# Where the second FFN's first weight operand lives, when its last three are fetched, and what is loaded ahead of its second product

## The chip, the cores and the metric

The kernel runs on one core of a Trainium2 chip. The metric is device time in microseconds (us) of one execution, from a set of timed runs; a profiled execution gives the trace. Engines: TensorE (PE, with its weight loads PEld), VectorE (DVE), ScalarE (ACT), GpSimd (POOL) and SyncE (SP). SP and POOL issue the DMAs here, each on a queue of its own.

## The reference, cut to what matters

```python
x = attention(q, k, v)              # linear attention with decay, 4 x 8 heads, 768 tokens, 64 wide
a = x @ w1; b = x @ w2              # first FFN: 3072 tokens, 512 -> 1024
x = ((a * b) @ w3) @ w_out          # 1024 -> 1024 -> 512
h = x @ w_in                        # second FFN: 512 -> 2048
g = h * (1 / (1 + exp(-1.702 * h)))
out = g @ w_out2                    # 2048 -> 512
```

The change touches the second FFN alone: `x @ w_in` with its gate, and `g @ w_out2`.

## The kernel before, in words

Every product is made of three matmuls (`mm3`), of a high and a low part of each operand. Both products of the second FFN are Strassen-like: seven block products P1 to P7 stand for the eight of a 2 x 2 block matrix.

**The block loop ahead of it.** The first FFN runs over six blocks of 512 tokens. In the last block each step f makes the products `gate(f)` (tile psm) and `mixed(f - 1)` (tile acc); `mixed(7)` is the last work. Its four results go through ACT or DVE into tiles st and by SP into DRAM (yd). During that block `operands(0, py)` cuts slice 0 of the tokens into the right operands yh, yl.

**Expand** (`x @ w_in`). Four slices s of 2 x 384 tokens, eight quads j each. Quad j of slice s needs the left operand `left[j]` (all seven weight combinations, 1792 KB, DRAM tensor sp) and makes P1, P5, then P4 of the quad before (`fourth`), then P6, P2, P3, P7: 7 x 6 matmuls. P1, P6, P7 and P4 go one after the other into the same PSUM bank a, and ACT copies the bank out after each (s1, u2, u3; after P4 the gate reads it), so that PE may go on in that bank only after the copy. The gates write the tile g (two buffers); DVE adds three more rows to it, and SP stores the whole of it to DRAM (gd, 1344 KB) in `fourth`. ACT does its work in program order: in a quad s1 copy, late gate g2 of the quad before, s5 copy, gate g1 of the quad before, u2 copy, gate g0, u3 copy, gate b12.

**Contract** (`g @ w_out2`). 21 turns (P1, P2, P6, P5, P3, P7, P4, three token ranges i of 512 each), 48 matmuls a turn. A turn reads its operand from gd in two halves of four k (low), ACT copies the high part of a half (h), DVE subtracts it from the low part. Turns n + 2 are loaded at turn n, the split of turn n + 1 stands behind the matmuls of turn n. Turn 0 (gd of slices 0 and 1) is loaded and split during slice 3 of Expand (`OPENING`), and the first half of turn 1 (slices 1 and 2) is loaded in its last quad. The other half of turn 1 is the first line of `contract`. Turn 2 needs all of gd of slice 3.

**Memory**, in bytes of a partition as the program before is laid out: a pool lays its tags one after another in the order of their first tile, and a tile waits for the tiles that lay there earlier, one by one. wmix of the first FFN 41,088 to 73,856 (read up to `mixed(7)` in every slot from 36,992 to 80,000), weights of `gate(4..7)` 73,856 to 106,624, hh and hl 106,624 to 114,816, tmp and st 114,816 to 123,008 (the last four results lie there until their stores have read them), xh and xl 123,008 to 139,392. The pool f then has eight slots of 14,336 from 8,320: slot 0 and 1 are free early, slots 2, 3 and 4 after `mixed(7)`, 5 and 6 a little ahead of it, slot 7 (108,672 to 123,008) after the stores of st. Left operand n goes to slot `SLOT[n]`, all eight asked for on POOL's queue at the start of Expand. Behind them in f1 lie g (123,008 and 133,760), b12, and the tiles s. In contract the pool f2 takes the place of f1 and of y: its first l1 tile (138,880 to 147,072), for the second half of turn 1, lies on the second g buffer, which the store of the last quad reads.

Of the kernel before, what the change touches and what calls it, by code (L numbers as in the profile page):

```python
# [16 lines left out]
P = 128  # L17
# [4 lines left out]
TB = 512  # L22
# [6 lines left out]
TS = 384  # L29
NS = NT // (2 * TS)  # L30
TU = 256
NQ = DG // (2 * P)
# [9 lines left out]
def tile_kernel(  # L42
# [14 lines left out]
    nc = tc.nc  # L57
# [339 lines left out]
    right = {}  # L397
# [66 lines left out]
    def left_parts(n, name, k):  # L464
        return [left[n][:, w, PART[name], k * P : (k + 1) * P] for w in range(2)]

    class Expand:

        def __init__(self, p, pf, py, ps):
            self.p, self.pf, self.py, self.ps = p, pf, py, ps  # L470
# [28 lines left out]
        def quad(self, s, j, step):  # L499
            a, e, c = (self.bank(x) for x in "aec")  # L500
            g = self.p.tile([P, 7, TS], F32, tag="g", bufs=2, name="g")
            b12 = self.p.tile([P, TS], F32, tag="b", bufs=2, name="b12")
            self.product(a, "P1", s, j, True)
            s1 = self.copy(a, "s1")
            if self.late:
                self.gated(*self.late.pop())
            self.product(e, "P5", s, j, True)
            s5 = self.copy(e, "s5")
            if self.open:
                self.fourth()  # L510
# [12 lines left out]
            self.gated(b12, u2)  # L523
            nc.vector.tensor_tensor(u3, u3, s5, ALU.add)
            self.late.append((g[:, 2], u3))
            nc.vector.tensor_tensor(g[:, 3], b12, g[:, 0], ALU.subtract)
            step(3)
            self.open = a, s, j, g, b12

        def run(self):  # L530
            self.late, self.open = [], None
# [3 lines left out]
            nxt = None  # L535
            for s in range(NS):

                for j in range(NQ):

                    def step(at):  # L540
                        nonlocal nxt
                        more = s + 1 < NS
                        if more and (j, at) == (2, 3):
                            nxt = operands(s + 1, self.py)
                            next(nxt)
                        elif more and (j, at) in NEXT:
                            next(nxt)
                        elif s and (j, at) == (0, 0):
                            next(nxt)
                        if not more and (j, at) in OPENING:  # L550
                            OPENING[j, at](self.pf)

                    self.quad(s, j, step)
            self.gated(*self.late.pop())
            self.fourth()

    NEXT = (4, 3), (5, 1), (5, 3), (6, 3), (7, 0), (7, 1), (7, 2), (7, 3)
# [2 lines left out]
    KH = NQ // 2  # L560
    low, high, ws = {}, {}, {}

    def slot(pf, n, shape, dtype=F32R):
        return pf.tile(shape, dtype, tag=f"op{SLOT[n]}", name=f"o{n}")

    def half_tile(p, kind, h, bufs):
        return p.tile([P, KH, TB], F32R, tag=f"{kind}{h}", bufs=bufs, name=f"{kind}{h}")

    def load_half(n, h, t):
        name, i = turns[n]  # L570
        low[n, h] = t
        at = 0
        while at < TB:
            s, t0 = divmod(i * TB + at, TS)
            m = min(TB - at, TS - t0)
            nc.sync.dma_start(
                t[:, :, at : at + m].bitcast(F32),
                gd[s][:, RIGHT[name], h * KH : (h + 1) * KH, t0 : t0 + m],
            )
            at += m  # L580

    def load_turn(n, p):
        if n < len(turns):
            for h in range(2):
                load_half(n, h, half_tile(p, "l", h, 3))

    def split_half(n, h, t, a=0, b=KH, copy=nc.scalar.copy):
        high[n, h] = t
        x = low[n, h][:, a:b]
        copy(t[:, a:b], x.bitcast(F32))  # L590
        nc.vector.tensor_tensor(x, x.bitcast(F32), t[:, a:b].bitcast(F32), ALU.subtract)  # L591

    def split_turn(n, p):
        if n < len(turns):
            for h in range(2):
                split_half(n, h, half_tile(p, "h", h, 2))

    def load_w(name, w, pf, at):
        t = slot(pf, at, [P, NQ, 256])
        ws.setdefault(name, []).append(t)  # L600
        nc.gpsimd.dma_start(t.bitcast(F32), sw[PART[name], :, w])

    def opening_split(h, a):
        def run(pf):
            if a == 0:
                high[0, h] = slot(pf, 2 + h, [P, KH, TB])
            split_half(0, h, high[0, h], a, a + 1)
        return run

    OPENING = {  # L610
        (1, 3): lambda pf: load_half(0, 0, slot(pf, 0, [P, KH, TB])),
        (2, 3): lambda pf: load_half(0, 1, slot(pf, 1, [P, KH, TB])),
        (5, 1): lambda pf: load_w("P1", 0, pf, 4),
        (6, 1): lambda pf: load_w("P1", 1, pf, 5),
        (7, 1): lambda pf: load_half(1, 0, slot(pf, 6, [P, KH, TB])),
    }
    OPENING |= {
        at: opening_split(n // KH, n % KH)
        for n, at in enumerate(
            ((3, 1), (3, 3), (4, 0), (4, 1), (4, 3), (5, 0), (5, 3), (6, 0))  # L620
        )
    }

    def contract(p, pf, ps):
        load_half(1, 1, half_tile(p, "l", 1, 3))
        w_at = (4, 5), (0, 1)
        u = [slot(pf, 7, [P, 3, 2, TB], F32)]

        def add(out, x, y):
            nc.vector.tensor_tensor(out, x, y, ALU.add)  # L630

        def store(x, h, i, q, value):
# [3 lines left out]
            while at < TB:  # L636
# [4 lines left out]
                nc.sync.dma_start(out[rows, to : to + m], t[:, at : at + m])  # L641
                at += m

        for n, (name, i) in enumerate(turns):
            r = n // 3
            load_turn(n + 2, p)
            if i == 0 and n and r + 1 < 7 or n == 1:
                nxt = turns[n + 3 - i][0]
                for w in range(2):
                    load_w(nxt, w, pf, w_at[(r + 1) % 2][w])  # L650
            if name == "P5" and i == 0:
                u += [slot(pf, x, [P, 3, 2, TB], F32) for x in (2, 3)]
            pq = [ps.tile([P, TB], F32, tag="m", bufs=6, name="m") for _ in range(2)]
            for q in range(2):
                for k in range(NQ):
                    mm3(
                        pq[q],
                        *(t[:, k, q * P : (q + 1) * P] for t in ws[name]),
                        high[n, k // KH][:, k % KH],
                        low[n, k // KH][:, k % KH],  # L660
                        k == 0,
                        k == NQ - 1,
                    )
# [20 lines left out]
    with tc.manual_schedule():  # L684
# [70 lines left out]
        with (  # L755
# [108 lines left out]
            late(*args)  # L864
        first.close()

        with tc.tile_pool(name="f", bufs=1, reuse_waits="tile") as pf:
            with (
                tc.tile_pool(name="f1", bufs=1, reuse_waits="tile") as p1,
                tc.tile_pool(name="psf1", bufs=1, space=PSUM, reuse_waits="tile") as ps1,  # L870
            ):
                Expand(p1, pf, py, ps1).run()
            third.close()
            with (
                tc.tile_pool(name="f2", bufs=1, side="right", reuse_waits="tile") as p2,
                tc.tile_pool(name="psf2", bufs=1, space=PSUM, reuse_waits="tile") as ps2,
            ):
                contract(p2, pf, ps2)


_OUTS = [((DM, NT), "float32")]
# [89 lines left out]
```

## Time and profile before

| what | us |
|---|---|
| median of 3 timed runs (1033.01 to 1040.57) | 1037.22 |
| profiled execution, device time | 1040.05 |
| its span in the trace | 1038.3 |
| PE busy in it | 987.5 |
| block loop's last matmul, start of Expand | 547.65 |
| last matmul of Expand, start of contract | 793.74 |

The device time is 1.75 us more than the span. Times in the rows count from the span's start. The mean granted TensorE clock is 0.988 of full speed (2.4 GHz).

### The profile page before, as it was taken

To read this page: it belongs to the slowest core of one execution; us is meant where nothing else is said; L and a number is where in the kernel's file an instruction comes from. 1 tells how busy PE (TensorE), PEld (TensorE's weight loads), DVE (VectorE), ACT (ScalarE), POOL (GpSimd) and SP (SyncE) were. 2 spreads that over 40 slices of the span, in tenths; PEclk is the share of its full clock that TensorE was granted. 3 is DMA by queue.
4 is the path that set the end of the run, shared out by engine and by line. 5 is a ranking of instruction groups with operands and counts; after the bars stand their busy time and mean duration, and the time that the engine had idled before them with its cause. 6 is when DMAs were issued, how large, how long until landed. Compare 5 with 4: busy or idle time off the path is not lost.

```text
span 1038.3 us, 14825 instructions
## 1 busy us (share of the span) xinstructions
PE 987.5 (95%) x5680; PEld 854.2 (82%) x5680; DVE 649.4 (63%) x1038; ACT 436.9 (42%) x831; POOL 32.1 (3%) x57
## 2 busy tenths in 40 slices
PE   4789999999999999999999899999999699999998
PEld 4568777888888888888889899999998488888886
DVE  4977888856777767733343485866764254645563
ACT  4766554434434343322113445445463332434230
POOL 3110000000000000000000000000000000000000
PEclk9999999999999999999999899999999899999999
DMA  8999654546766767641319847556578978868971
GB/s 323 340 405 351 213 182 151 164 154 205 241 222 232 244 214 224 199 152 41 124 31 407 321 178 256 213 202 230 196 257 293 336 255 279 285 234 281 316 257 58
DMA packets 138806, 240.40 MB, mean 232 GB/s; under 512 B 7024, under 2 KB 111600, under 8 KB 132976
## 3 DMA queue, kind: packets, MB, share of 16 engines
q1 hardware_dynamic: 131968, 184.94, 52.6%
q0 software_dynamic: 6768, 54.53, 13.7%
q8 instruction: 44, 0.72, 0.3%
q14 instruction: 26, 0.21, 0.1%
HBM read 148.21 MB, written 91.23 MB: 231 GB/s over the span
## 4 chain that ended last, share of the span: by engine, by line
PE 80%; DMA 8%; DVE 7%; issue 2%; ACT 2%; POOL 0%; SPq 0%; DVEq 0%; ACTq 0%; POOLq 0%
PE psm L231 8%; PE psm L230 8%; PE psm L229 8%; PE m L230 7%; PE m L231 7%; PE m L229 7%; PE acc L230 4%; PE acc L229 4%; PE acc L231 4%; DMA gd<-g 3%; DMA qkv<-in_qkv_dram 3%; PE a L229 3%; PE a L231 3%; PE a L230 3%; PE e L229 2%
## 5 line engine op out<-in xcount | busy, mean ns | idle before, releaser
L231 PE MATMUL psm<-xh,wl 128*128 128x512 f32 x384 | 149.6, 390 | 1.2 <-DVE wl L119 1.2
L230 PE MATMUL psm<-xl,wh 128*128 128x512 f32 x384 | 149.5, 389 | 0.0
L229 PE MATMUL psm<-xh,wh 128*128 128x512 f32 x384 | 149.5, 389 | 0.0
L229 PE MATMUL m<-h,o 128*128 128x512 f32 x320 | 125.5, 392 | 8.1 <-ACT h L590 8.1
L231 PE MATMUL m<-h,o 128*128 128x512 f32 x320 | 125.0, 391 | 0.0
L230 PE MATMUL m<-l,o 128*128 128x512 f32 x312 | 122.2, 392 | 1.5 <-DVE l L591 1.5
L590 ACT CAST h<-l 128x2048 fp32r<-128x2048 f32 x39 | 74.1, 1912 | 102.0 <-DMA l<-gd 58.4
L591 DVE TENSOR_TENSOR l<-l,h 128x2048 fp32r<-128x2048 f32 x39 | 88.0, 2286 | 35.6 <-ACT h L590 35.5
L801 DVE TENSOR_TENSOR tmp<-tmp,psm 128x512 f32<-128x512 f32 x48 | 32.9, 686 | 103.9 <-PE psm L231 92.9
L229 PE MATMUL a<-yh,op 128*128 128x384 f32 x256 | 87.0, 340 | 8.9 <-ACT u L478 8.9
L230 PE MATMUL a<-yl,op 128*128 128x384 f32 x256 | 86.4, 337 | 0.0
L231 PE MATMUL a<-yh,op 128*128 128x384 f32 x256 | 86.4, 337 | 0.0
L231 PEld LDWEIGHTS psm<-xh,wl 128*128 128x128 f32 x384 | 72.1, 188 | 16.5 <-DVE wl L119 1.6
L229 PEld LDWEIGHTS psm<-xh,wh 128*128 128x128 f32 x384 | 72.1, 188 | 15.0
L230 PEld LDWEIGHTS psm<-xl,wh 128*128 128x128 f32 x384 | 72.1, 188 | 14.9
L782 ACT CAST hh<-tmp 128x512 fp32r<-128x512 f32 x48 | 29.8, 620 | 124.1 <-DVE tmp L801 124.1
L229 PEld LDWEIGHTS m<-h,o 128*128 128x128 f32 x320 | 60.5, 189 | 21.2 <-ACT h L590 8.5
L229 PE MATMUL acc<-hh,wh 128*128 128x512 f32 x192 | 74.7, 389 | 0.0
L230 PE MATMUL acc<-hl,wh 128*128 128x512 f32 x192 | 74.7, 389 | 0.0
L231 PE MATMUL acc<-hh,wl 128*128 128x512 f32 x192 | 74.7, 389 | 0.0
L231 PEld LDWEIGHTS m<-h,o 128*128 128x128 f32 x320 | 60.5, 189 | 12.4
L230 PEld LDWEIGHTS m<-l,o 128*128 128x128 f32 x312 | 59.0, 189 | 14.3 <-DVE l L591 2.0
(109 smaller groups left out, 1817.6 us busy)
## 6 DMA issues: line engine op xcount, KB each, us to landing
gd<-g SPq DMA_DIRECT2D x32, 1344.0 KB, 5.9
qkv<-in_qkv_dram POOLq DMA_DIRECT2D x23, 1024.0 KB, 8.1
l<-gd SPq DMA_DIRECT2D x26, 768.0 KB, 8.2
raw<-in_w_dram SPq DMA_DIRECT2D x32, 512.0 KB, 4.7
op<-sp POOLq DMA_DIRECT2D x8, 1792.0 KB, 11.0
o<-sw POOLq DMA_DIRECT2D x14, 1024.0 KB, 7.5
l<-gd SPq DMA_DIRECT2D x26, 512.0 KB, 5.6
raw<-in_wo_dram SPq DMA_DIRECT2D x24, 512.0 KB, 5.6
```

Of the source, the lines that this page charges most:

```text
L229: nc.tensor.matmul(ps, wh, xh, start=start, stop=False, skip_group_check=True)
L230: nc.tensor.matmul(ps, wh, xl, start=False, stop=False, skip_group_check=True)
L231: nc.tensor.matmul(ps, wl, xh, start=False, stop=stop, skip_group_check=True)
L590: copy(t[:, a:b], x.bitcast(F32))
L591: nc.vector.tensor_tensor(x, x.bitcast(F32), t[:, a:b].bitcast(F32), ALU.subtract)
L782: nc.scalar.copy(hi, t)
L801: nc.vector.tensor_tensor(t, t, pb, ALU.mult)
```

## The change: what it does

Left operand 0 gets a pool of its own ("e", at the right end of memory), opened in the last block of the first FFN, and is fetched there. Operands 1 to 4 are fetched on POOL's queue at the start of Expand, into the first four places of the pool f, which now has seven; operands 5, 6 and 7 are asked for on SP's queue, each right behind the store of g of quads 0, 1 and 2 of slice 0. g and the other tiles of f1 therefore lie 14,336 lower, and so do y and f2, below e.

In a quad the copy u3 of P7 now stands on ACT ahead of the gates g0 and b12; the late gate g2 and three of the four subtractions form `third`, behind P1's copy of the next quad. One more buffer for the tiles s.

During slice 3 turn 0's low halves go into slots 0 and 1, its high halves into slots 2 and 3, and each of these four slots also takes a quarter (two k) of turn 1, so that the whole of turn 1 is loaded ahead; turn 0's high parts are copied by DVE in place of ACT. In contract the tile ua lies in f2, the weights of P2 are asked for at turn 0 on SP's queue behind the loads of turn 2 (before: turn 1, POOL's queue).

```diff
-    SLOT = 0, 1, 5, 6, 2, 3, 4, 7
-    def left_tile(pool, slot):
-        return pool.tile([P, 2, 7, 256], F32R, tag=f"op{slot}", name="op")
-    def fetch_left(n, t):
-        left[n] = t
-        nc.gpsimd.dma_start(t.rearrange("p a b c -> p a (b c)").bitcast(F32), sp[n])
+    SLOT = "e", 0, 1, 5, 6, 2, 3, 4
+    pools = {}
+    def slot(n, shape):
+        x = SLOT[n]
+        return pools[x == "e"].tile(shape, F32R, tag=f"op{x}", name="op")
+    def fetch_left(n, queue=nc.gpsimd):
+        t = left[n] = slot(n, [P, 2, 7, 256])
+        queue.dma_start(t.rearrange("p a b c -> p a (b c)").bitcast(F32), sp[n])
...
-            t = self.p.tile([P, TS], F32, tag="s", bufs=5, name=name)
+            t = self.p.tile([P, TS], F32, tag="s", bufs=6, name=name)
...
+        def third(self):
+            self.gated(*self.late)
+            g, b12 = self.open[-2:]
+            for x, y, z in ((3, b12, g[:, 0]), (5, g[:, 2], b12), (4, g[:, 2], g[:, 3])):
+                nc.vector.tensor_tensor(g[:, x], y, z, ALU.subtract)
+
         def fourth(self):
-            a, s, j, g, b12 = self.open
+            a, s, j, g, _ = self.open
             self.product(a, "P4", s, j)
             self.gated(g[:, 1], a)
-            for x, y, z in ((5, g[:, 2], b12), (4, g[:, 2], g[:, 3]), (6, g[:, 1], g[:, 4])):
-                nc.vector.tensor_tensor(g[:, x], y, z, ALU.subtract)
+            nc.vector.tensor_tensor(g[:, 6], g[:, 1], g[:, 4], ALU.subtract)
             nc.sync.dma_start(gd[s][:, :, j], g)
+            if s == 0 and j + 5 < NQ:
+                fetch_left(j + 5, nc.sync)
             self.open = None
...
             s1 = self.copy(a, "s1")
-            if self.late:
-                self.gated(*self.late.pop())
+            if self.open:
+                self.third()
...
             nc.vector.tensor_tensor(s1, c, s1, ALU.add)
-            self.gated(g[:, 0], s1)
...
             u3 = self.copy(a, "u3")
+            self.gated(g[:, 0], s1)
             self.gated(b12, u2)
             nc.vector.tensor_tensor(u3, u3, s5, ALU.add)
-            self.late.append((g[:, 2], u3))
-            nc.vector.tensor_tensor(g[:, 3], b12, g[:, 0], ALU.subtract)
+            self.late = g[:, 2], u3
...
-            homes = [left_tile(self.pf, x) for x in range(NQ)]
-            for n in range(NQ):
-                fetch_left(n, homes[SLOT[n]])
+            for n in range(1, 5):
+                fetch_left(n)
...
+    def opening_slot(n):
+        t = slot(n, [P, KH + 2, TB])
+        if n < 2:
+            load(0, n * KH, (n + 1) * KH, t[:, :KH])
+        else:
+            high.setdefault(0, []).append(t[:, :KH])
+        k = (4, 6, 0, 2)[n]
+        load(1, k, k + 2, t[:, KH:])
+
+    def opening_split(k):
+        hi, lo = high[0][k // KH][:, k % KH], low_of(0, k)
+        nc.vector.tensor_copy(hi, lo.bitcast(F32))
+        nc.vector.tensor_tensor(lo, lo.bitcast(F32), hi.bitcast(F32), ALU.subtract)
+
+    OPENING = {(n + 1, 1): [lambda n=n: opening_slot(n)] for n in range(4)}
+    for n in range(2):
+        OPENING[5 + n, 1] = [lambda n=n: load_w("P1", n, 4 + n)]
+    for k, at in enumerate(
+        ((3, 1), (3, 2), (3, 3), (4, 0), (4, 1), (4, 3), (5, 1), (5, 3))
+    ):
+        OPENING.setdefault(at, []).append(lambda k=k: opening_split(k))
...
-    def contract(p, pf, ps):
-        load_half(1, 1, half_tile(p, "l", 1, 3))
-        w_at = (4, 5), (0, 1)
-        u = [slot(pf, 7, [P, 3, 2, TB], F32)]
+    def contract(p, ps):
...
+        u = [p.tile([P, 3, 2, TB], F32, name="ua")]
         for n, (name, i) in enumerate(turns):
             r = n // 3
             load_turn(n + 2, p)
-            if i == 0 and n and r + 1 < 7 or n == 1:
-                nxt = turns[n + 3 - i][0]
+            if i == 0 and r + 1 < 7:
                 for w in range(2):
-                    load_w(nxt, w, pf, w_at[(r + 1) % 2][w])
+                    queue = nc.gpsimd if r else nc.sync
+                    load_w(turns[n + 3][0], w, (6, 4)[r % 2] + w, queue)
...
                         second.close()
+                        pools[True] = ctx.enter_context(
+                            tc.tile_pool(name="e", bufs=1, side="right", reuse_waits="tile")
+                        )
+                        fetch_left(0)
```

## Rows read from the trace of the kernel before

**Rows 1.** Waits of PE over the whole run: total us, times, longest

```profile
PE a L229 <- ACT u L478: 8.9, 5, 5.3
PE m L229 <- ACT h L590: 8.1, 1, 8.1
...
PE m L230 <- DVE l L591: 1.5, 1, 1.5
```

**Rows 2.** Stretches: us, busy of PE, PEld, DVE, ACT, POOL, clock, DMA share, GB/s

```profile
560.00:583.00 23.00, 17.69 (x86) 17.37 (x85) 7.45 (x14) 7.38 (x17) 0.53 (x1) 0.85 1.03 404
...
803.00:820.00 17.00, 7.38 (x27) 5.37 (x26) 3.94 (x3) 5.11 (x5) 0.53 (x1) 0.73 1.01 345
```

**Rows 3.** Timeline of PE, 547 to 582: start, us, instruction, [idle before]

```profile
547.65 0.33 PE L229 MATMUL a<-yh,op 128*128 128x384 f32 x1
...
570.38 0.34 PE L231 MATMUL e<-yh,op 128*128 128x384 f32 x1
576.03 0.69 PE L229 MATMUL a<-yh,op 128*128 128x384 f32 x1 [5.31 <-ACT u L478]
...
581.96 0.35 PE L229 MATMUL e<-yh,op 128*128 128x384 f32 x1
```

**Rows 4.** Timeline of ACT, 562 to 577

```profile
565.61 0.48 ACT L478 COPY u<-a 128x384 f32<-128x384 f32 x1 [0.60 <-PE a L231]
575.09 0.52 ACT L488 ACTIVATE g<-s 128x384 f32<-128x384 f32 x1 [9.00 <-DMA gd<-g]
```

**Rows 5.** Chain of work that ended last, 500 to 600: start, us, what

```profile
558.34 16.66 DMA gd<-g
```

**Rows 6.** Timeline of POOL, 500 to 585: the fetches of left operands

```profile
509.80 0.53 POOL L462 DMA_DIRECT2D op<-sp  x1 [394.43 <-PE psm L231]
...
548.11 1.70 POOL L462 DMA_DIRECT2D op<-sp  x3 [2.42 <-PE acc L231]
```

**Rows 7.** Landing of stores yd<-st: the last, issued at 548.6; twenty before 540

```profile
DMA to landing us min/median/max: 23.0/23.0/23.0
...
DMA to landing us min/median/max: 2.3/2.9/6.1
```

**Rows 8.** Timeline of PE, 620 to 625

```profile
623.41 0.44 PE L229 MATMUL a<-yh,op 128*128 128x384 f32 x1 [0.69 <-ACT u L478]
```

**Rows 9.** Timeline of PE, 790 to 822

```profile
792.57 0.45 PE L229 MATMUL a<-yh,op 128*128 128x384 f32 x1 [1.53 <-ACT u L478]
...
807.15 0.39 PE L231 MATMUL m<-h,o 128*128 128x512 f32 x1
...
821.02 0.39 PE L231 MATMUL m<-h,o 128*128 128x512 f32 x1
```

**Rows 10.** Chain of work that ended last, 780 to 822

```profile
780.75 10.80 DMA gd<-g
...
795.42 6.93 DMA gd<-g
...
802.78 10.82 DMA l<-gd
...
813.68 1.91 ACT h L590
...
815.61 2.30 DVE l L591
```

**Rows 11.** Timeline of ACT, 775 to 850: the split of turn 2's second half

```profile
819.66 1.90 ACT L590 CAST h<-l 128x2048 fp32r<-128x2048 f32 x1 [1.07 <-DMA l<-gd]
```

**Rows 12.** SP's timeline at 745; landing of the store issued at 744.8

```profile
745.39 1.83 SPq L576 DMA_DIRECT2D o<-gd  x2
...
DMA to landing us min/median/max: 6.3/6.3/6.3
```

**Rows 13.** Groups of DVE instructions by shape, 547 to 850: busy, mean ns

```profile
L423 DVE CAST yh<-yr 128x768 fp32r<-128x768 f32 x15 | 8.3, 552 | 0.0
...
L591 DVE TENSOR_TENSOR o<-o,o 128x512 fp32r<-128x512 f32 x8 | 5.5, 690 | 1.4 <-ACT o L590 1.4
```

More of the change, by code (lines that the diff above doesn't have):

```diff
@@ L467, in tile_kernel, with __init__ @@
     class Expand:
-        def __init__(self, p, pf, py, ps):
-            self.p, self.pf, self.py, self.ps = p, pf, py, ps
+        def __init__(self, p, py, ps):
+            self.p, self.py, self.ps = p, py, ps
         def bank(self, kind):
@@ L530, in run @@
         def run(self):
-            self.late, self.open = [], None
-            homes = [left_tile(self.pf, x) for x in range(NQ)]
-            for n in range(NQ):
-                fetch_left(n, homes[SLOT[n]])
-            nxt = None
+            self.open = nxt = None
+            for n in range(1, 5):
+                fetch_left(n)
             for s in range(NS):
@@ L550, in step @@
                         if not more and (j, at) in OPENING:
-                            OPENING[j, at](self.pf)
+                            for run in OPENING[j, at]:
+                                run()
                     self.quad(s, j, step)
-            self.gated(*self.late.pop())
+            self.third()
             self.fourth()
@@ L561, in tile_kernel, with low_of, load @@
     low, high, ws = {}, {}, {}
[L563 to L569, printed above, removed]
+    def low_of(n, k):
+        return next(t[:, k - a] for a, b, t in low[n] if a <= k < b)
+    def load(n, a, b, t):
         name, i = turns[n]
-        low[n, h] = t
+        low.setdefault(n, []).append((a, b, t))
         at = 0
@@ L577, in load_half @@
                 t[:, :, at : at + m].bitcast(F32),
-                gd[s][:, RIGHT[name], h * KH : (h + 1) * KH, t0 : t0 + m],
+                gd[s][:, RIGHT[name], a:b, t0 : t0 + m],
             )
@@ L584, in load_turn @@
             for h in range(2):
[L585 to L591, printed above, removed]
-    def split_turn(n, p):
[L594 to L599, printed above, removed]
-        ws.setdefault(name, []).append(t)
-        nc.gpsimd.dma_start(t.bitcast(F32), sw[PART[name], :, w])
@@ L603, in opening_split @@
[L603 to L622, printed above, removed]
-    def contract(p, pf, ps):
-        load_half(1, 1, half_tile(p, "l", 1, 3))
-        w_at = (4, 5), (0, 1)
-        u = [slot(pf, 7, [P, 3, 2, TB], F32)]
+                t = p.tile([P, KH, TB], F32R, tag=f"l{h}", bufs=3, name=f"l{h}")
+                load(n, h * KH, (h + 1) * KH, t)
+    def split_turn(n, p):
+        if n >= len(turns):
+            return
+        high[n] = [
+            p.tile([P, KH, TB], F32R, tag=f"h{h}", bufs=2, name=f"h{h}") for h in range(2)
+        ]
+        for a, b, x in sorted(low[n], key=lambda t: t[0]):
+            hi = high[n][a // KH][:, a % KH : (b - 1) % KH + 1]
+            nc.scalar.copy(hi, x.bitcast(F32))
+            nc.vector.tensor_tensor(x, x.bitcast(F32), hi.bitcast(F32), ALU.subtract)
@@ new lines, in load_w @@
+    def load_w(name, w, at, queue=nc.gpsimd):
+        t = slot(at, [P, NQ, 256])
+        ws.setdefault(name, []).append(t)
+        queue.dma_start(t.bitcast(F32), sw[PART[name], :, w])
+    def opening_slot(n):
[10 more added lines that the diff above has]
+        nc.vector.tensor_tensor(lo, lo.bitcast(F32), hi.bitcast(F32), ALU.subtract)
@@ L646, in contract @@
             load_turn(n + 2, p)
-            if i == 0 and n and r + 1 < 7 or n == 1:
-                nxt = turns[n + 3 - i][0]
+            if i == 0 and r + 1 < 7:
                 for w in range(2):
-                    load_w(nxt, w, pf, w_at[(r + 1) % 2][w])
+                    queue = nc.gpsimd if r else nc.sync
+                    load_w(turns[n + 3][0], w, (6, 4)[r % 2] + w, queue)
             if name == "P5" and i == 0:
-                u += [slot(pf, x, [P, 3, 2, TB], F32) for x in (2, 3)]
+                u += [slot(x, [P, 3, 2, TB]).bitcast(F32) for x in (2, 3)]
             pq = [ps.tile([P, TB], F32, tag="m", bufs=6, name="m") for _ in range(2)]
@@ L658, in contract @@
                         *(t[:, k, q * P : (q + 1) * P] for t in ws[name]),
-                        high[n, k // KH][:, k % KH],
-                        low[n, k // KH][:, k % KH],
+                        high[n][k // KH][:, k % KH],
+                        low_of(n, k),
                         k == 0,
@@ L865, in tile_kernel @@
         first.close()
-        with tc.tile_pool(name="f", bufs=1, reuse_waits="tile") as pf:
+        with tc.tile_pool(name="f", bufs=1, reuse_waits="tile") as pools[False]:
             with (
@@ L871, in tile_kernel @@
             ):
-                Expand(p1, pf, py, ps1).run()
+                Expand(p1, py, ps1).run()
             third.close()
@@ L877, in tile_kernel @@
             ):
-                contract(p2, pf, ps2)
+                contract(p2, ps2)
 _OUTS = [((DM, NT), "float32")]
```

## The prediction, made before the changed kernel was timed

> **What bounds the kernel now.** TensorE does: it is busy 987.5 us of a 1038.3 us span, so a change pays only where PE stands still or runs at the lower clock. I read the waits of PE over the whole run first. In the second FFN they are few: five waits for the copy of bank a, 8.9 us together with one of 5.3, and in contract 8.1 and 1.5 us for the split of an operand [rows 1]. Then the stretches around the long ones: in 560 to 583 the granted clock is 0.85 of full speed, in 803 to 820 it is 0.73, and in both the DMA engines are full, at 404 and 345 GB/s [rows 2]. So each long wait costs twice, once as idle time and once as matmuls at 1.2 GHz behind it, and both are DMA waits at bottom. After 826 PE waits for nothing.
>
> **The first wait, at the start of Expand.** PE issues 132 matmuls from 547.65 up to the one at 570.38, one every 0.1735 us. The next starts at 576.03, and the one at 581.96 is 18 later [rows 3]. At the full rate it would have started at 570.55 + 18 x 0.1735 = 573.68. The loss is 8.28 us: 5.3 idle and the rest slow clock. Its cause is read backwards: PE waits for u3's copy, which stands on ACT behind gate g0 of quad 2, which waits 9.00 us for the store of quad 0's g, whose buffer it takes [rows 4]. That store was issued at 558.34 and landed 16.66 us later [rows 5], beside the left operands that POOL had asked for at 548.11 and before [rows 6]. The stores of the first FFN's result suffered the same: 23.0 us for the last, where the median of earlier ones is 2.9 [rows 7].
>
> After the change operand 0 is asked for at the start of the last block, 8 x 36 matmuls or 65 us before PE needs it, on a queue with nothing else in it; I cost that at nothing. 1 and 2 find their places free at about 510, as two fetches do now, and only 3 and 4 (places 36,992 to 65,664, under wmix, read up to the end of the block loop) are asked for at 548.1. That is 3.67 MB, at 404 GB/s some 9 us; with 3 us to start they are through at about 560.5. The store of quad 0 shares the engines with them for 2 us, not for 17, and should land by 566. How late may it land? With u3's copy ahead, PE can go on through P7, P1, P5 and P4, and stands only at P6 of the next quad, which needs s1's copy. Quad 3 starts at 547.65 + 3 x 7.29 = 569.5 (7.29 is 42 x 0.1735), P6 is 18 matmuls later, at 572.6; ahead of it on ACT stand g0, b12 and s1, some 0.5 us each [rows 4]. So g0 must start by 571.1: five us of slack. The three later fetches are on SP's queue behind stores of quads 0, 1, 2, issued at about 559, 566 and 573, and needed at 584, 591 and 599; stores, fetches and the load of slice 1 up to there are 8 MB, 20 us of the queue. Nothing else on SP is held, since places 5 to 7 are free by 548. I take the whole **8.28 us** as gained.
>
> A wait is added here. g now starts at 108,672, over the last st tiles, so g0 of quad 0 on ACT waits for the stores of yd. Queued behind it are b12 and s1's copy of quad 1, and PE waits for that at P6: by the same count g0 must start by 554.94 + 3.12 - 1.5 = 556.6. The last of these stores is issued at 548.6. Alone it takes 2.9 us and lands at 551.5; that is the lower end, and costs nothing. Beside five fetches it took 23.0 us. With two fetches in flight and the queue empty before 548 I bound it by the end of both, 561: 4.3 us of idle PE and, by the first wait, 2.8 of slow clock, 7 together. The fetch of 509.80 has its engines free and needs some 3 us before data flow, so most of the stores' bytes go first: I take 0, and keep 7 for the range.
>
> **Three short waits and one at the end of Expand.** In quad 0 of slices 1 to 3 PE stands 0.69 us, three times alike [rows 8]: DVE is full of operand splits, s1's sum is late, g0 waits for it and u3's copy for g0. With the copy ahead this goes: 3 x 0.69 = **2.07 us**. At the end of slice 3 the same order costs 1.53 us [rows 9], where g0 waits for the store issued at 780.75, which took 10.80 [rows 10]: **1.53 us**. What is late next in both is s1's copy, with 1 us to spare or more, and in the last quad there is no next s1. `third` only moves three subtractions on DVE; none feeds PE. The extra DVE copies for turn 0 are eight, each under the 0.55 us of a 768-wide cast, beside subtractions of 0.69 that stand there now [rows 13]: at most 3 x 1.24 = 3.7 us in quad 3 and in quad 4. Quads 7 and 0 of the earlier slices carry five wider splits, and cost PE only the 0.69 above. PE reads none of it before turn 0. I take 0; without that cover s1's sum is late by at most such 0.69 in two quads, 1.4 us.
>
> **The transition.** Contract runs without a break from 793.74; its 60th matmul is at 807.15, so one takes 13.41 / 59 = 0.2273 us, and PE stands from 807.38 [rows 9]. The chain there is plain: the last store of g issued at 795.42 lands after 6.93; only then is the second half of turn 1 asked for, since its tile lies on that g; it lands at 813.6, and 1.91 us of cast on ACT and 2.30 of subtraction on DVE come before PE may go on [rows 10]. The matmul at 821.02 is the ninth behind the gap; without it, it would have started at 807.38 + 8 x 0.227 = 809.20. The loss is 11.82 us. After the change turn 1 has landed in quads 1 to 4 of slice 3; its four splits, each half of 1.91 and 2.30, need only that ACT and DVE are through with Expand (795) and that h lies on free memory (y tiles of P1, P5, P6, P7, last read at 791): ready by 800, and turn 1 begins at 803.1.
>
> What is late next is turn 2. It needs the same last store, at 802.4 at the latest. Turn 2 begins at 792.2 + 2 x 10.9 = 814.0 and reads its second half at 816.7. Before, 5.2 MB (a half of turn 1, two weight fetches of POOL, turn 2) were through at 819.66 [rows 11]: 17.3 us, 303 GB/s. Now turn 2's 2.1 MB stand first: 802.4 + 6.9 = 809.3, with 4.2 of split 813.5. Slack 3 us for the second half, 4 for the first. Then P2's weights and turn 3, 6.3 MB since 802.4: 823.2, split 827.4, needed at 825.0 + 2.7 = 827.7. So turn 3 is just in time, and I leave 0 to 2 us for it. Gain **11.82 us**.
>
> **The sum**, against the profiled execution: 8.28 + 2.07 + 1.53 + 11.82 = 23.7; 1040.05 - 23.7 = 1016.4. That execution lies 2.8 us above the median of the timed runs, 1037.22, from which the same sum gives 1013.5. I predict 1015.
>
> **Rival 1: turn 2 is late, so half of the transition stays.** If the loads do not land in the order asked for, and turn 2 shares the engines with P2's weights and turns 3 and 4 behind it, it lands no earlier than now, at 819.66, and PE stands at 816.7 until 819.66 + 4.2 = 823.9: 7 us, and 1 to 2 at the lower clock. 1016.4 + 8.5 = 1025. For it: SP now issues fourteen loads in a row. Against: before, turn 1's half, asked for first, landed 6 us ahead of turn 2's. Chance 0.14.
>
> **Rival 2: the stores of the first FFN hold the first g.** Price 7 us at my bound, 1023.5. If they take 23.0 us as now, g0 waits to 571.7, PE stands 15 us and the clock takes 2.8: 1034, which is no change. It decides from a landing at 556.6 on. Chance 0.10, mostly near the first number.
>
> **Rival 3, slower: the store of g is slowed by what is asked for right behind it.** If the queue shares the engines between a store and the next request as SP and POOL share them now, every store with a big request behind it takes the 17 us of rows 5; g0 of the second quad after it waits, s1's copy behind it, and PE pays about 8.3 us each time, the price of the first wait. There are five such stores: quads 0, 1, 2 of slice 0 and quads 0 and 1 of slice 3. 5 x 8.3 = 41.4 against 23.7 gained: 1058. It decides from a landing time of 12.8 us on (558.34 to 571.1). Against it: at 744.8 a store of g had a 1 MB load issued right behind it at 745.39 on the same queue, and landed in 6.3 us [rows 12]. Chance 0.04. The Trainium skill (DMA: Bandwidth & Descriptors, "Issuing engines are not separate DMA queues") says that DMAs run on the same 16 engines and interleave whichever engine started them, so that issuing on another one saves only issue time. By that rule alone moving three fetches from POOL to SP would protect no store; the 6.3 us beside the 16.66 speak against reading it so, though no row has a left operand behind a store on SP's queue.
>
> **How the numbers follow.** Forecast as summed, 1010 to 1020: 0.66. Rival 1: 0.14. Rival 2: 0.10. Rival 3: 0.04. Something not seen, around 1030 to 1040: 0.06. The low end is the sum taken from the lowest run shown, 1009; the high end takes in rivals 1 and 2 at their likely prices: 1026. A change of 1%, 10.4 us, is about what a measurement of this kernel can tell from none. Above 1026.8 lie rival 3, the far end of rival 2 and half of the unseen: faster 0.88, same 0.08, slower 0.04.
>
> **What would show it.** In the profile after: no wait of PE for u in Expand, and clock 1.00 over its first 40 us; the first store of g landing in about 6 us; the first g0 at about 555 waiting for PE or DVE, not for yd; at the end turn 0, 1 and 2 without a break, and the loads of turn 2 landing 7 us after the last store of g. Wrong would be: ACT waiting for yd past 556.6, a wait of PE for h or l at turn 2 or 3, or stores of g of over 12 us in slice 0 or 3.

## The result, and the profile after

The changed kernel takes 1022.25 us (median of 4 runs, 1021.58 to 1024.06), the kernel before 1036.2 in the same series (4 runs, 1033.01 to 1040.57): a ratio of 0.9865, 95% interval 0.9826 to 0.9905. It is 14 us faster. I had said 1015 and 1009 to 1026: the direction and the range hold, and the time is 7 us above the 1015. The profiled execution took 1022.59 us (span 1020.8), 17.5 below the one of before (1040.05). The runs of the kernel before scatter over 7.5 to 9.4 us in every series (1032 to 1042 in all), and its three profiles (1040.05, 1038.41, 1038.71) are all in the upper half; why, no trace here shows, and the medians are the fairer measure.

The waits of PE come first, as before (total us, times, longest). Of the rows that stood there [rows 1], those for h and l in contract are gone, and u went from 8.9 us in five waits to one of 0.6. The wait for s is new.

```profile
PE a L229 <- ACT s L480: 3.6, 2, 2.2
...
PE a L229 <- ACT u L480: 0.6, 1, 0.6
```

The stretches (us; busy PE, PEld, DVE, ACT, POOL; clock, DMA share, GB/s) answer to [rows 2]. The granted clock is 1.00 in all four, and PE is full in 560 to 583 and in 803 to 820. What is lost now lies in the stretches that I had not listed, 547 to 560 and 583 to 606.

```profile
547.00:560.00 13.00, 11.55 (x65) 11.04 (x64) 4.05 (x8) 4.74 (x11) 1.04 (x2) 1.00 0.90 343
560.00:583.00 23.00, 23.00 (x135) 23.00 (x134) 12.57 (x24) 11.42 (x26) 0.00 (x0) 1.00 0.94 345
583.00:606.00 23.00, 20.80 (x118) 20.16 (x117) 15.93 (x27) 9.58 (x23) 0.00 (x0) 1.00 0.88 335
...
803.00:820.00 17.00, 17.00 (x77) 14.08 (x76) 8.31 (x4) 7.29 (x6) 0.00 (x0) 1.00 1.07 363
```

PE's timeline (start, us, instruction, [idle before]) has the three waits that are left. The first two are new; the third is what remains of the 1.53 us at 792.57 [rows 9].

```profile
559.12 0.44 PE L229 MATMUL a<-yh,op 128*128 128x384 f32 x1 [1.45 <-ACT s L480]
...
590.67 0.45 PE L229 MATMUL a<-yh,op 128*128 128x384 f32 x1 [2.16 <-ACT s L480]
...
786.55 0.45 PE L229 MATMUL a<-yh,op 128*128 128x384 f32 x1 [0.57 <-ACT u L480]
```

ACT's timeline tells why, read as [rows 4] were: ahead of s1's copy stands gate g0, and g0 waits for a store. At 557.77 it is the last result of the first FFN, whose tile st lay where g now lies; at 589.32 it is the store of quad 2's g, two quads earlier, whose buffer it takes. The last two rows are the splits of turn 2 in contract: its halves landed at 800.1 and 803.1, where before the second came at 819.6 [rows 11].

```profile
557.77 0.52 ACT L490 ACTIVATE g<-s 128x384 f32<-128x384 f32 x1 [2.70 <-DMA yd<-st]
...
589.32 0.52 ACT L490 ACTIVATE g<-s 128x384 f32<-128x384 f32 x1 [3.42 <-DMA gd<-g]
...
800.19 1.91 ACT L600 CAST h<-l 128x2048 fp32r<-128x2048 f32 x1 [0.79 <-DMA l<-gd]
803.15 1.91 ACT L600 CAST h<-l 128x2048 fp32r<-128x2048 f32 x1 [1.04 <-DMA l<-gd]
```

The chain of work that ended last (start, us, what) has just these two transfers between 545 and 605; in the place of the store that took 16.66 us [rows 5] stand these.

```profile
549.04 8.62 DMA yd<-st
...
575.09 14.14 DMA gd<-g
```

To see how the time of the whole splits, I counted each phase of PE against its matmuls at the full rate (Expand 1344 x 0.1735 us, contract 1008 x 0.2273, both rates from the prediction). "Lost" is the rest, with the slow clock in it; of contract some 3.9 us is the end of the kernel.

| us | before | after | forecast gain | measured gain |
|---|---|---|---|---|
| first matmul of Expand at | 547.65 | 548.12 | 0 | -0.5 |
| lost in Expand | 12.9 | 6.4 | 11.9 | 6.5 |
| lost in contract | 15.4 | 4.0 | 11.8 | 11.5 |
| together | | | 23.7 | 17.5 |

So contract gave what was forecast, and Expand 5.4 us less. The first row moves between 547.1 and 550.4 in the profiles shown below, the kernel before's among them, so 0.5 is nothing of the change.

### The profile page after: what moved, and what is told of

It is laid out like the page before. It is cut to its first block, busy times and chain, and to the rows that moved or that the text cites. A ratio compares the mean times of both kernels' runs of the same rounds, so it can differ in the third digit from the quotient of the medians.

```text
span 1020.8 us, 14838 instructions
## 1 busy us (share of the span) xinstructions
PE 984.3 (96%) x5680; PEld 851.3 (83%) x5680; DVE 656.3 (64%) x1048; ACT 429.2 (42%) x825; POOL 29.8 (3%) x52
## 4 chain that ended last, share of the span: by engine, by line
PE 83%; DVE 7%; DMA 6%; issue 2%; ACT 1%; POOL 0%; DVEq 0%; ACTq 0%; POOLq 0%
PE psm L231 8%; PE psm L230 8%; PE psm L229 8%; PE m L230 7%; PE m L231 7%; PE m L229 7%; PE acc L230 4%; PE acc L229 4%; PE acc L231 4%; DMA qkv<-in_qkv_dram 4%; PE a L229 3%; PE a L231 3%; PE a L230 3%; PE e L229 2%; PE e L231 2%
## 5 line engine op out<-in xcount | busy, mean ns | idle before, releaser
L229 PE MATMUL m<-h,op 128*128 128x512 f32 x320 | 124.5, 389 | 0.0
L231 PE MATMUL m<-h,op 128*128 128x512 f32 x320 | 124.5, 389 | 0.0
L230 PE MATMUL m<-l,op 128*128 128x512 f32 x304 | 118.3, 389 | 0.0
L231 PEld LDWEIGHTS psm<-xh,wl 128*128 128x128 f32 x384 | 72.1, 188 | 16.6 <-DVE wl L119 1.6
L480 ACT COPY u<-a 128x384 f32<-128x384 f32 x64 | 30.7, 480 | 96.9 <-PE a L231 96.9
L229 PEld LDWEIGHTS m<-h,op 128*128 128x128 f32 x320 | 60.1, 188 | 12.6
L231 PEld LDWEIGHTS m<-h,op 128*128 128x128 f32 x320 | 60.1, 188 | 12.4
```

The source lines that it names most:

```text
L229: nc.tensor.matmul(ps, wh, xh, start=start, stop=False, skip_group_check=True)
L230: nc.tensor.matmul(ps, wh, xl, start=False, stop=False, skip_group_check=True)
L231: nc.tensor.matmul(ps, wl, xh, start=False, stop=stop, skip_group_check=True)
```

## Experiments: the start of Expand

**All fetches on POOL again.** Of the change everything stays but the asking one by one.

```diff
-            if s == 0 and j + 5 < NQ:
-                fetch_left(j + 5, nc.sync)
...
-            for n in range(1, 5):
+            for n in range(1, NQ):
                 fetch_left(n)
```

> The changed kernel with operands 5, 6 and 7 asked for on POOL's queue right behind 1 to 4, at the end of the block loop, in place of one by one on SP's. Theory A (POOL's fetches hold back what SP has asked for, and g now lies on the stores of yd): the last store of yd lands 20 us or more after its issue, g0 of quad 0 starts at about 570 and not at 557.8, PE stands 12 to 15 us at P6 of quad 1 with slow clock behind it; 1034 to 1040, no faster than before. Rival (the order of asking matters little, since all bytes go through the same engines before they are needed): the store lands in under 12 us, and the time stays within 4 us of 1022.

Measured: 1028.73 us, 0.9932 of before (0.9906 to 0.9957). Both theories miss. ACT's timeline shows the last st landing hardly later than in the changed kernel (8.93 us after its issue against 8.62), so that g0 waits 3.01 us; but the store of quad 0's g took 17.82 us (start, us, what, from the chain), and the gate behind it waits 7.79. PE is idle 6.5 us there and loses 9.0 with the slow clock.

```profile
563.84 17.82 DMA gd<-g
...
560.36 0.52 ACT L490 ACTIVATE g<-s 128x384 f32<-128x384 f32 x1 [3.01 <-DMA yd<-st]
...
581.74 0.52 ACT L490 ACTIVATE g<-s 128x384 f32<-128x384 f32 x1 [7.79 <-DMA gd<-g]
```

It follows that asking one by one on SP's queue is what protects the store of g, worth 5 to 6.5 us of time (the edit moves queue and moment together, so which of the two does it is not shown); and that the stores of yd suffer as much from POOL's first two fetches as from five.

**Operands 3 and 4 on SP's queue,** behind the stores of yd, where POOL had asked for them beside these stores.

```diff
-                fetch_left(n)
+                fetch_left(n, nc.gpsimd if n < 3 else nc.sync)
```

> The changed kernel with operands 3 and 4 asked for on SP's queue as well, behind the four stores of yd, and not on POOL's. Theory A (what stands ahead on the same queue goes first, what comes by the other queue is shared in): the last store of yd lands 3 to 4 us after its issue and not 8.6, g0 of quad 0 does not wait, PE does not stand at quad 1; 1.7 us faster than the changed kernel, some 1020.5. Rival (the engines are simply full from 549 on, whoever asked): the store still takes over 7 us and the wait stays, or one queue alone moves fewer bytes and the second wait grows by as much; 1022 or more.

**Operands 6 and 7 a quad later,** so that operand 6 is not ahead of quad 2's store.

```diff
-            if s == 0 and j + 5 < NQ:
-                fetch_left(j + 5, nc.sync)
+            if s == 0 and j in (0, 2, 3):
+                fetch_left({0: 5, 2: 6, 3: 7}[j], nc.sync)
```

> The changed kernel with operand 6 asked for behind the store of quad 2 and operand 7 behind that of quad 3 (before: quads 1 and 2), so that the store of quad 2 no longer stands behind operand 6 on SP's queue. Theory A (the second wait is the queue ahead of that store): the store lands in about 10 us and not 14.1, the wait of 2.4 us goes, and operand 7 lands at about 597, just before PE needs it at 600; 1019.5 to 1020. Rival (too many bytes for the time, 8 MB in 25 us, whatever the order): the wait moves to the next store or to operand 7, 2 us or more; 1022 to 1024.

**Both edits together,** and the changed kernel beside them:

> Both edits together. Theory A: neither wait is left, 4 us faster than the changed kernel, some 1018. Rival: one queue with 18 MB from 547 to 597 is behind all along; a wait of 3 us or more in some quad of slice 0, 1021 or more.

> The changed kernel, unchanged, beside the three below on one chip. Both theories: about 1022, with PE standing 1.5 to 2 us at P6 of quad 1 (g0 behind the last store of yd) and 2 to 3 us at P6 of a quad about five later (g0 behind the store of quad 2's g).

Measured, all on one chip against 1036.05 for before (landings in us; those of the changed kernel from its first profile, its loss in Expand from both):

| kernel | median us | ratio, 95% | last yd store lands after | stores of quads 0, 1, 2, 3 | lost in Expand |
|---|---|---|---|---|---|
| changed | 1023.59 | 0.987 (0.9838 to 0.9903) | 8.6 | 7.1, 9.6, 14.1, 14.4 | 6.4 and 7.7 |
| 3 and 4 on SP | 1020.72 | 0.9845 (0.9815 to 0.9875) | 4.1 | 7.2, 8.1, 13.1, 13.8 | 4.0 |
| 6 and 7 later | 1019.42 | 0.9837 (0.9807 to 0.9868) | 8.7 | 7.4, 10.1, 10.2, 10.6 | 3.8 |
| both | 1018.52 | 0.9825 (0.9794 to 0.9856) | 4.3 | 9.0, 10.2, 10.2, 11.2 | 2.45 |

Theory A came out in all three, though 3 and 4 on SP gained 2.9 us where 1.7 was expected. Each edit takes away one wait and leaves the other. With 3 and 4 on SP the stores of yd land as the first line below says, no gate waits for them, and what is left stands behind the stores of quads 2 and 3:

```profile
DMA to landing us min/median/max: 2.4/2.8/4.1
...
586.74 0.52 ACT L490 ACTIVATE g<-s 128x384 f32<-128x384 f32 x1 [2.37 <-DMA gd<-g]
594.71 0.53 ACT L490 ACTIVATE g<-s 128x384 f32<-128x384 f32 x1 [1.59 <-DMA gd<-g]
```

With 6 and 7 later, of the two only the wait for yd is left:

```profile
559.59 0.52 ACT L490 ACTIVATE g<-s 128x384 f32<-128x384 f32 x1 [2.83 <-DMA yd<-st]
```

And with both, the waits of PE in all of Expand are down to 1.0 us:

```profile
PE a L229 <- ACT u L480: 0.6, 1, 0.6
PE a L229 <- ACT s L480: 0.4, 1, 0.4
```

That version is faster than both kernels: 5.1 us below the changed one on the same chip. The slowest run of all three edits (1022.15) is below the changed kernel's fastest there (1023.17).

## Experiments: the order of gate and copy

**The gate ahead of u3's copy again,** in the changed kernel:

```diff
             nc.vector.tensor_tensor(s1, c, s1, ALU.add)
+            self.gated(g[:, 0], s1)
...
             u3 = self.copy(a, "u3")
-            self.gated(g[:, 0], s1)
```

> The changed kernel with gate g0 back at its old place, behind s1's sum and so ahead of u3's copy on ACT; all else as changed. Theory A (the order of these two lets PE go on for another 18 matmuls when g0 waits, and keeps DVE's lateness from PE): the three waits in quad 0 grow from 0.4 to 1.0 again, and the waits of g0 for yd and for the store of quad 2 reach PE earlier: yd is needed at about 553 and lands at 557.7, so PE stands 3 to 4 us at quad 1; 3 to 7 us slower than the changed kernel, 1025 to 1030. Rival (the order is worth only the three short waits): 1 to 2 us, 1023 to 1025.

Measured: 1028.43 us, 0.9924 of before (0.9893 to 0.9955), against 0.9865 and 0.987 with the copy ahead: by the medians the order is worth 5 to 6 us here, more than the 3.6 that I had summed for it. By the profiles it is less: Expand loses 10.8 us, against 6.4 and 7.7 in the changed kernel's two, 3 to 4.5 us more, and the rest stands ahead of Expand, where nothing was edited. PE's waits in Expand show where it comes from. All are for u now, and the short ones are back (three losses of 0.97 us, start to start, as before), but g0's two waits for yd and gd also reach PE a copy earlier: they cost 2.35 and 4.71 us where the changed kernel loses 1.73 and 2.45 (1.7 and 4.09 in its second profile). At the end of Expand the old order costs almost nothing: PE waits 0.62 us there, against 0.57 with the new one.

```profile
792.40 0.44 PE L229 MATMUL a<-yh,op 128*128 128x384 f32 x1 [0.62 <-ACT u L480]
...
PE a L229 <- ACT u L480: 7.7, 6, 2.9
```

**The copy ahead of the gate, alone,** in the kernel before: the same two lines the other way.

> The kernel before with one edit: g0 moved behind u3's copy on ACT. Theory A: the three waits of 1.0 shrink to 0.4, that at the end from 1.8 to 0.9, and the long wait at the start of Expand, where the store lands 17 us after its issue and g0 may wait for 12.8 now and not 11.4, by 1.4; 3 to 4.5 us faster than before, 1032 to 1033.5. Rival (what PE gains there, it waits at P6 for s1's copy instead): under 2 us.

Measured: 1037.9 us, 1.002 of before (0.9995 to 1.0046): no gain. Its profile has Expand losing 10.25 us where the three profiles of before lose 12.9 to 13.1, so 2.7 us should show (0.7 at the long wait, 0.35 at each short one, 1.0 at the end); the runs (1035.75 to 1042.31) do not show it. This run is inconclusive as to time. What the trace does show is that the long wait hardly moves: the store of quad 0 takes 16.59 us, and PE is idle 4.61 us behind s1's copy where it was 5.31 behind u3's. Alone, the order gives 0.7 us there; the gain needs the store to land earlier.

```profile
574.49 0.52 ACT L488 ACTIVATE g<-s 128x384 f32<-128x384 f32 x1 [5.81 <-DMA gd<-g]
```

## Experiments: the transition

Two more profiles of the kernel before, since its transition is to be compared with single profiles:

> The kernel before, unchanged, profiled once more. Theory A: the 4 us by which the measured gain (1036.2 to 1022.25, 14.0 us) falls short of the gain between the two profiled executions (1040.05 to 1022.59, 17.5 us) lies in the long wait at the start of Expand, whose length goes with how far POOL's fetches delay one store and so differs from run to run; a second profile then shows that wait, idle and slow clock together, some 2 to 6 us shorter than 8.3, or as long, with the other waits (0.69 three times, 1.5, and 11.8 at the transition) the same. Theory B: the difference lies ahead of the first FFN's end, in the waits for qkv; then the start of Expand is 8.3 us again and the first matmul of Expand moves by some us from 547.65.

> The kernel before, a third profile. In two so far the loss at the start of Expand was 8.4 and 8.5 us, that at the transition 11.8 and 9.9. Theory A (what makes runs of this kernel differ by up to 8 us are these waits and their slow clock): at least one of the two differs again by 1 us or more in the direction of this run's time. Rival: both as in one of the earlier profiles, and the time differs by the waits of attention for qkv.

They took 1038.41 and 1038.71 us, with 8.45 and 8.33 us lost at the first long wait, and 9.89 and 9.58 at the transition. The prediction's profile had 11.80 there: the upper end of three. So what differs most from the first profile is the transition, not the long wait at the start of Expand, as the first theory A had it, nor the first matmul of Expand (547.65 and 547.55), as theory B had it; between the second and the third nothing moved by 1 us. The chain of the third profile has the load that ends last at 7.88 us, where the prediction's row had 10.82 [rows 10]:

```profile
802.86 7.88 DMA l<-gd
```

**The second half of turn 1 asked for late again,** into the tile on the second g, the rest as changed (called half_late in what follows):

```diff
-        load(1, k, k + 2, t[:, KH:])
+        if n > 1:
+            load(1, k, k + 2, t[:, KH:])
...
         u = [p.tile([P, 3, 2, TB], F32, name="ua")]
+        load(1, KH, NQ, p.tile([P, KH, TB], F32R, tag="l1", bufs=3, name="l1"))
```

> The changed kernel with the second half of turn 1 not loaded ahead but asked for as the first line of contract, into an l tile that lies on the last g, as before. Theory A (the 11.8 us of the transition came from asking late): PE stands again behind k = 3 of turn 1, 8 to 12 us with the slow clock; 1031 to 1034. Rival (it came from POOL's two weight fetches, which shared the engines with that half; they now stand on SP's queue behind the loads): the half lands 5 us after the last store of g instead of 11, PE stands 2 to 4 us, 1024 to 1027.

Measured: 1029.78 us, 0.9937 (0.9916 to 0.9957), 6 to 7.5 us above the changed kernel. Not all of the old loss is back: the transition loses 4.97 us, and what else that profile has over the changed kernel's, 2.8 us, stands ahead of Expand and in its first slice, where nothing was edited. The result lies between the two theories: the load is as quick as the rival has it, the time is out of both ranges. The chain is that of [rows 10]:

```profile
792.36 5.38 DMA gd<-g
...
798.29 5.18 DMA l<-gd
...
803.49 1.91 ACT h L600
```

**The same, with P2's weights again at turn 1 on POOL's queue:**

```diff
-            if i == 0 and r + 1 < 7:
+            if i == 0 and n and r + 1 < 7 or n == 1:
                 for w in range(2):
-                    queue = nc.gpsimd if r else nc.sync
-                    load_w(turns[n + 3][0], w, (6, 4)[r % 2] + w, queue)
+                    load_w(turns[n + 3 - i][0], w, (0, 4)[r % 2] + w)
```

> As half_late (the second half of turn 1 asked for at the start of contract, into a tile on the last g), and P2's weights back on POOL's queue at turn 1, into the places of turn 0's low halves, as before. Half_late alone lost 5.0 us at the transition, the kernel before 10 to 12. Theory A (the other 5 to 7 us are these two fetches of POOL, which share the engines with the late half): the half lands 8 to 11 us after it is asked for and not 5, the loss at the transition is 9 to 12 us again, 1034 to 1037. Rival (the rest came from something else, as the load of turn 1's first half in the last quad of Expand): 5 to 6 us, 1029 to 1031.

Measured: 1028.97 us, 0.9919 (0.989 to 0.9948). In the profile the same load takes 8.11 us, beside a fetch that POOL asks for 0.14 us behind it, and the transition loses 9.15, nearly as much as in the kernel before. The time is the rival's:

```profile
794.65 8.11 DMA l<-gd
...
794.79 0.53 POOL L606 DMA_DIRECT2D op<-sw  x1 [20.77 <-PE m L230]
```

So by the profiles about half of the old loss came from asking late, and the other half from POOL's two weight fetches (1024 KB each), which were under way beside the late half. The times don't confirm the second part: the two kernels' ratios agree within their intervals. Their two profiles took 1030.19 and 1030.22 us because the one with the longer transition began Expand 2.2 us earlier and lost 1.9 less in it. That division stays a reading of single profiles.

**One tile off g,** in the kernel before: a small tile ahead of the late half moves that half from the second g buffer onto tiles s, so that its load need not wait for the last store.

```diff
     def contract(p, pf, ps):
+        p.tile([P, TB], F32, tag="o", bufs=4, name="c")
         load_half(1, 1, half_tile(p, "l", 1, 3))
```

> The kernel before with one line added: a tile of tag o is taken first in f2, so that the l tile for the second half of turn 1 no longer lies on the last g, but on the tiles s, and need not wait for g's store. Nothing else of the change. Theory A (the transition's loss comes from the memory under one tile): the load is issued at about 796 in place of 802.4, lands by 803 to 805, PE does not stand at turn 1 and at most 2 us at turn 2; 8 to 11 us faster than before, 1025 to 1029. Rival (the load must be made during Expand, since at the end the engines are full): it lands hardly sooner than 813, gain under 4 us.

Measured: 1032.84 us, 0.9973 (0.9954 to 0.9993): 3 to 4 us, the rival's gain, though the load landed at 805.9, near theory A's. The load was asked for 7 us earlier, at 795.63, but beside the last store and then POOL's fetches it took 10.29 us, and the transition still loses 5.38. The hidden dependence on g's memory was real; removing it alone gives back about half.

## Why the prediction was right, and where it was not

**The transition, 11.82 us: right in what it removes.** No wait of PE for h or l is left, and contract is 11.46 us shorter. Rival 1 did not come about: SP's queue (start, us) issues the loads of turn 2 at once behind the last store, which landed 5.4 us after its issue, then P2's weights, then turn 3.

```profile
789.55 0.51 SPq L503 DMA_DIRECT2D gd<-g  x1
794.99 2.02 SPq L580 DMA_DIRECT2D l<-gd  x4
797.05 0.98 SPq L606 DMA_DIRECT2D op<-sw  x2
```

Turn 2's halves landed 5.2 and 8.2 us after 794.9, where 6.9 was forecast, with 9 us to spare at the second, or 5 behind its split. The account of the cause was too simple, though: I put all of the loss down to the late request, and the profile of the half asked for late loses 5.0 without POOL's fetches. And the price was that of one profile: the other two had 9.9 and 9.6 to give back.

**The old wait at the start of Expand, 8.28 us: right in cause, and gone.** The store of quad 0 landed in 7.1 us, and with all fetches on POOL it took 17.82 and the wait came back. What came in its place has two parts, and they are the two steps that failed. Both show in signs that the prediction had named as wrong: ACT waited for yd until 557.77, past 556.6, and two stores of slice 0 took over 12 us (14.1 and 14.4).

**The stores of yd, taken at 0: mis-sized; Rival 2's mechanism, at about a quarter of its price.** Of the four stores the landing after issue is

```profile
DMA to landing us min/median/max: 2.4/2.9/8.6
```

and only the last, issued at 549.04, is slow: POOL had asked for operand 3 half a microsecond earlier and asked for operand 4 at the same moment.

```profile
548.58 1.04 POOL L464 DMA_DIRECT2D op<-sp  x2 [37.26 <-PE acc L231]
```

It landed at 557.7, 1.1 us past the 556.6 from which I had said that the rival decides, and PE lost 1.73 us. The 556.6 was too late by one product: it counts 42 matmuls for quad 0, which makes no P4 and has 36 (the 132 up to 570.38 are 36 + 42 + 42 + 12). With 36 it is 555.5, or 556.0 in a run whose Expand begins 0.5 us later, and 557.7 is 1.7 past that. The step "most of the stores' bytes go first, I take 0" failed; three of four did go first. The range between my two ends (551.5 and 561) held the landing, and the value that I took from it did not. The Trainium skill (DMA: Bandwidth & Descriptors, "Queues, rings and completion order") says that an engine with work on several queues serves them in turn, packet by packet; by that the store would get every other turn and take some twice the 2.9 us of its row, an estimate of 5.8. The trace agrees in direction, not in size: 8.6 us beside two fetches on POOL's queue, 4.1 with the same fetches behind it on SP's. The Trainium skill's rule which I had weighed, that the issuing engine decides only issue time ("Issuing engines are not separate DMA queues" on the same page), is not borne out: these two kernels differ in the queue of operands 3 and 4 alone, and so in their place behind the stores, and the second is 2.9 us faster. Its fetches are also asked for later, 0.4 us after the last store and not 0.5 ahead of it; no run asks for them that late on POOL's queue, so how much is the queue and how much the moment stays open.

**The queue's bytes counted for the operands and not for the store: failed.** I had "8 MB, 20 us of the queue" and asked only whether operands 5 to 7 come in time. They do, although what that sentence lists (three stores, three operands, slice 1) is 11.2 MB, 28 us at its rate. But the store of quad 2 stands in the same queue, and has to land in 12.8 us by my own figure for Rival 3, in 11.8 with quad 0 counted right. SP's timeline has what is ahead of it:

```profile
561.25 0.58 SPq L503 DMA_DIRECT2D gd<-g  x1
562.04 0.48 SPq L464 DMA_DIRECT2D op<-sp  x1
567.82 0.56 SPq L503 DMA_DIRECT2D gd<-g  x1
568.55 0.58 SPq L464 DMA_DIRECT2D op<-sp  x1
569.19 3.91 SPq L405 DMA_DIRECT2D yr<-yd  x2
575.09 2.57 SPq L503 DMA_DIRECT2D gd<-g  x1
```

Three stores of 1344 KB, two operands of 1792 KB and slice 1's loads of 1536 KB make 9.37 MB from 561.25 to the landing at 589.2: 28 us, 335 GB/s, with a queue that had work all along: operand 5 landed 11.9 us after its issue, operand 6 13.2. At the 404 GB/s that I had used, a figure of a stretch in which POOL's queue moved data too, it would have been 23 us, and the store would have landed at 584.5, in time. So the store took 14.1 us because of what was asked for ahead of it, and PE lost 2.45 us. That is not Rival 3, which had stores slowed by requests behind them: quad 0's had operand 5 right behind it and landed in 7.1. Asked for a quad later, right behind this store and not ahead of it, operand 6 leaves the store 10.2 us, and the wait is gone. No rival of the prediction had this cause.

**The short waits, 2.07, and the end of Expand, 1.53: mostly right.** The three went from 0.97 us each, start to start, to 0.39: 1.74 gained. At the end of Expand 0.57 us of 1.53 remain: there neither P1 nor another product stands between P7 and the last P4, so the copy u3 itself is waited for, with nothing ahead of it. The prediction named the absent s1 and overlooked this. Nor was the order the only way to this gain: with the old one put back PE waits 0.62 there, for the store that g0 waits for took 10.80 us before and 9.1 in that run. The 0.39 that is left of each short wait is s1's copy, for which I had 1 us to spare: DVE still ends s1's sum late, at 619.08 in slice 1, and g0 and b12 stand ahead of the copy. What the extra copies for turn 0 were to cost, nothing, stands: PE loses nothing in quads 3 and 4 of slice 3.

**The sum.** Forecast 23.7; less 5.4 in Expand, 0.4 in contract and 0.5 at its start makes the 17.5 of the profiles. The two new waits, 4.2 us, are most of the 5.4, and the version that removes them is at 1018.5. The other part of the distance to the median is the base: 1015 rests on a profiled execution near the top of its runs, whose transition, 11.80, two more profiles put at 9.6 and 9.9. That the range held is in part luck: its high end was made for rivals 1 and 2, and a wait that neither had took up some of it. Taken back one at a time, the fetches one by one, the order and the early turn 1 cost 5 to 6.5, 5 to 6 and 6 to 7.5 us, 16 to 20 together against a gain of 14: these prices do not add up to the whole, and each holds some of the drift ahead of what was edited. Operand 0's own place, the sixth buffer and DVE's copies were not taken back alone.

## What to carry to other kernels

When a fetch moves behind a store on one queue, the store of the next step stands behind that fetch: count the bytes ahead of each store against the time at which its buffer is wanted, at the rate measured for that queue. A large fetch on another queue slowed the stores asked for at the same time, so a store that frees a buffer was quicker here when the fetch was issued behind it on its own queue (7.1 us against 16.6 to 17.8). In an engine that works in program order, put what frees a PSUM bank ahead of what may wait for a DMA: in the changed kernel that was worth 5 to 6 us by the medians and 3 to 4.5 by the profiles, some of it on waits that were not there before; in the kernel before, alone, no gain showed in the time.

## What the runs showed of the hardware that was not expected

A 1344 KB store took 5.4 us on a quiet queue, 7.1 with 1792 KB right behind it, 14.1 with two operands, two stores and a load ahead of it, and 16.6 to 17.8 beside fetches on the other queue. Issuing itself was slower with more ahead in the queue: the instruction for a store, 0.56 us at 567.82, took 2.57 at 575.09, and 0.56 again at 576.94 in the kernel that asks for operand 6 behind that store. That the bytes ahead are the reason is a reading.

The same short wait may cost the clock or not. After 2.16 us of idle PE at 590.67 the changed kernel kept the granted clock at 1.00 in 583 to 606; in its second profile the wait was as long, the clock in that stretch was 0.93, and the loss 4.09 us in place of 2.45; what decides, no run shows:

```profile
583.00:606.00 23.00, 20.79 (x111) 20.47 (x110) 14.12 (x24) 8.68 (x21) 0.00 (x0) 0.93 0.85 325
```
